# Converting float64 weights on Trainium2: the exponent is lowered on ScalarE, and one of VectorE's three steps goes

## The chip, the cores and the metric

One Trainium2 chip, of which this kernel uses one core. TensorE (PE) multiplies matrices, VectorE (DVE), ScalarE (ACT) and GpSimd (POOL) work element by element, and SyncE (SP) issues most transfers. Each engine works through its own list of instructions in order; semaphores make one wait for another. The metric is the time of one execution on the device in microseconds (us); lower is better.

## The reference

Pooled attention, then two feed-forward layers, over 8 x 576 = 4608 tokens of width 512:

```python
k_p, v_p = mean of k, v over groups of 8 positions
x = softmax(q @ k_p.T / 8) @ v_p
g, val = x @ w_gate, x @ w_val                     # 512 x 1536 each
x = (g * sigmoid(g) * val) @ w_out                 # 1536 x 512
h = x @ w_in                                       # 512 x 2048
out = (P(h) / (Q(h) + 1e-6)) @ w_out2              # 2048 x 512; P, Q small polynomials in h and |h|
```

The five weight matrices arrive in the accelerator's memory as float64; q, k and v are float32.

## The kernel before

Every matrix product is made of three products of TensorE's rounded float32 type: each float32 operand is split into a high part (the rounded value, by ScalarE) and a low part (the rest, by a subtraction), and `mm3` adds high x high, low x high and high x low. A product of one 128 x 128 weight block with 512 tokens is one matmul; 12 such matmuls (four blocks, three terms) are called *a product* below.

The tokens are worked on in nine blocks of 512. The program's stages, in order:

- **Start**: attention of block 0, while the first weights arrive.
- **Stage 0** (`j == 0`, L774 to L819): block 0 goes through the first feed-forward layer in 12 turns (`f`), each one of 128 hidden columns: the products `gp` (gate) and `vp` (value), then the output product `acc` of the turn before. Meanwhile attention for block 1 is placed in turns 5 to 11 (`place`). In this stage the weights of the first layer are converted as they are used: `first.step(6)` stands three times in a turn (L789, L796, L807), once for each of the turn's three weight tiles.
- **Stages 1 and 2**: blocks 1 and 2 in the same way, with the weights kept. GpSimd makes sums of the weights that a later stage wants; from stage 1 on, the second layer's weights are converted in half tiles (`Halves`, L176) and put back into memory.
- **Pair stage** (L902 to L976): the other six blocks, in three pairs of 12 turns, with weights streamed from memory; attention and the second layer's conversions go on beside.
- **The rest**: the output products of the pairs, and the second layer. No weights are converted any more.

A float64 is two 32-bit words. The conversion to float32 (`conversion`, L102) makes the float32's bits out of the high word's and adds the top bits of the low word:

1. `words()` on ScalarE: the magnitude of the high word, read as a float32, into tile `t` (L110); and the low word as an integer, times 2^-29 (L111), which leaves its top three bits.
2. `bits`, on VectorE: the maximum of `t` and a least value (L120), so that a tiny weight's exponent doesn't wrap; a shift left by 3 and a mask that drops the top two bits (L121); and `select` (L114), which takes the top two bits of the high word itself and joins them to the shifted rest.
3. GpSimd adds the low word's three bits (L117).

`Weights.step` (L143) keeps three tiles in flight, one in each part: it subtracts for the low half of the tile that is last (L149, VectorE), starts `words()` of a new one, runs the VectorE part for the one in the middle, and rounds the high half of the third (L165, ScalarE). So between L114 of a tile and its L149 there is GpSimd's addition and ScalarE's rounding, and the product that needs the tile's low half waits for L149. The names are those of the trace: `rawg`, `rawv`, `rawo` for the words of a gate, value and output tile, `tg`, `tv`, `to` for their `t`, `wg`, `wv`, `wo` for what is made of them, `rawi` and `rawo` with 256 columns for the half tiles. The `t` of some tiles and the loads of k, v and q share a pool of six buffers (`ldp`, tag `ld`), so a load waits until L114 has read an older `t`.

There are 36 conversions of 128 x 512 in the start and stage 0, and 64 of 128 x 256 from stage 1 to the end of the pair stage. In a half tile's turn `second.begin()`, `.middle()` and `.end()` hold ScalarE's words, VectorE's bits, and the split.

Of the kernel before, what the change touches and what calls it, by code (L numbers as in the profile page):

```python
# [10 lines left out]
F32 = mybir.dt.float32  # L11
F32R = mybir.dt.float32r
U32 = mybir.dt.uint32
AF = mybir.ActivationFunctionType
ALU = mybir.AluOpType
# [48 lines left out]
def attention_gated_rational(  # L64
# [4 lines left out]
    nc = tc.nc  # L69
# [11 lines left out]
    def f32(ap):  # L81
        return ap.bitcast(F32)
# [14 lines left out]

    LEAST = float(np.uint32(0x38000000).view(np.float32))  # L100

    def conversion(key, raw, n, spare, t=None):  # L102

        hi_word, lo_word = raw[:, :, 1], raw[:, :, 0]
        if t is None:
            t = ldp.tile([P, 512], F32, tag="ld", name=f"t{key}")[:, :n]
        tu = t.bitcast(U32)

        def words():
            nc.scalar.activation(t, hi_word.bitcast(F32), AF.Abs)  # L110
            nc.scalar.activation(lo_word, lo_word, AF.Copy, scale=2.0 ** -29)  # L111

        def select():
            nc.vector.scalar_tensor_tensor(  # L114
                hi_word, hi_word, 0xC0000000, tu, op0=ALU.bitwise_and, op1=ALU.bitwise_or
            )
            nc.gpsimd.tensor_tensor(tu if spare else hi_word, hi_word, lo_word, op=ALU.add)  # L117

        bits = [
            lambda: nc.vector.tensor_scalar(t, t, LEAST, None, op0=ALU.max),  # L120
            lambda: nc.vector.tensor_scalar(  # L121
                tu, tu, 3, 0x3FFFFFFF, op0=ALU.logical_shift_left, op1=ALU.bitwise_and
            ),
            select,
        ]
        return words, bits, t if spare else f32(hi_word)

    class Weights:
# [14 lines left out]
        def step(self, ahead, eng=None):  # L143
            begun = None
            middle, rounded, last = self.stages
            if last:
                key, spare, _, t = last
                w = self.done[key]
                (eng or nc.vector).tensor_tensor(w[:, 1, :], t, f32(w[:, 0, :]), op=ALU.subtract)  # L149
                live["w"] -= not spare  # L150
            if self.raws:
                key, raw, spare = self.raws.pop(0)
                words, bits, t = conversion(key, raw, 512, spare)
                words()
                begun = key, spare, bits, t
            if middle:
                for fn in middle[2]:
                    fn()
                live["w"] -= middle[1]
            if rounded:  # L160
                live["w"] += 1
                assert live["w"] <= WSLOTS
                key, t = rounded[0], rounded[3]
                w = self.done[key] = wslot(f"w{key}")
                nc.scalar.activation(w[:, 0, :], t, AF.Copy)  # L165
            self.stages = [begun, middle, rounded]
            while self.next < len(self.items) and len(self.raws) < ahead:
                if live["w"] + (self.next < self.spare or any(x and not x[1] for x in self.stages)) >= WSLOTS:
                    break
                self.load()  # L170
# [5 lines left out]
    class Halves:  # L176
# [26 lines left out]
        def begin(self, n=1, more=1):  # L203
            self.store()
            for _ in range(more):
                self.load()
            self.now = []
            for key, h, tile_, raw in [self.raw.pop(0) for _ in range(min(n, len(self.raw)))]:
                t = f32(tile_[:, 512:768])
                words, bits, _ = conversion(f"{key}_{h}", raw, 256, True, t)  # L210
                words()
                self.now.append((key, h, tile_, t, bits))
# [803 lines left out]
    def hidden_part(p, key, k):  # L1016
        while order_h and len(ahead) < 3:
            nxt = order_h[0]
            if nxt[0] != p and nxt[2] == 0 and k < NK - 1:
                break  # L1020
            ahead.append(hidden_sum(*order_h.pop(0)))
        t = ring_tile(f"h{p}{key}_{k}")
        split(t[:, 0, :], t[:, 1, :], ahead.pop(0))
        return t
# [3 lines left out]
    for p, (j1, j2) in enumerate(PAIRS):  # L1028
# [36 lines left out]
        for i, (ow, key) in enumerate(zip(O_ORDER, TOKENS)):  # L1065
# [5 lines left out]
            for k in range(NK):  # L1071
                t = hidden_part(p, key, k)
# [29 lines left out]
    with tc.tile_pool(name="p2", bufs=1, reuse_waits="tile") as p2:  # L1102
# [31 lines left out]
        for n, (j, f) in enumerate(its):  # L1134
# [11 lines left out]
            t = p2.tile([P, BLK], F32, tag="t", name=f"t{n}")  # L1146
# [93 lines left out]
```

## Time and profile before

| | us |
|---|---|
| median of 3 runs | 1798.62 (1796.67 to 1802.75) |
| the profiled execution: its own time | 1798.48 |
| the profiled execution: span from first to last instruction | 1796.7 |
| PE busy | 1743.1 (97%) |
| DVE busy | 1404.0 (78%) |
| ACT busy | 1135.4 (63%) |
| POOL busy | 345.4 (19%) |

Busy times are sums over the span; an engine that is busy for 78% of all the time can be busy for all of one stage. The ends of matmuls in the trace are modelled, so a PE that is shown busy may still be issuing less than it could. The mean granted clock of TensorE is 0.996 of 2.4 GHz.

### The profile page before, as it was taken

How to read it: one execution, taken by the hardware profiler on the slowest of the kernel's cores; microseconds unless marked ns; L12 is line 12 of the kernel's file. 1: busy time of each engine (PE TensorE's matmuls, PEld its weight loads, DVE VectorE, ACT ScalarE, POOL GpSimd, SP SyncE). 2: the span in 40 equal slices, each digit the busy share in tenths (PEclk: the TensorE clock that was granted, in tenths of full speed). 3: DMA queues.
4: the chain of work that ended last, by engine and by line, in shares of the span. 5: the costliest groups of instructions: out<-in, count | busy, mean ns of one | idle time of the engine just before them, and what ended most of it. 6: DMA issues, size and time to landing. Idle time of an engine off the chain costs nothing.

```text
span 1796.7 us, 23824 instructions
## 1 busy us (share of the span) xinstructions
PE 1743.1 (97%) x8212; PEld 1423.5 (79%) x8212; DVE 1404.0 (78%) x2333; ACT 1135.4 (63%) x1994; POOL 345.4 (19%) x492
## 2 busy tenths in 40 slices
PE   6898999999999999999999999999999999999998
PEld 5677877787887887887888788888888888888887
DVE  7997665548777676546777898989898989898987
ACT  5676455546665766435455676777677777767775
POOL 3344555542454344210000000000000000000000
PEclk9999999999999999999999999999999999999999
DMA  7631756559999898999826601010101010101000
GB/s 256 215 109 59 226 184 238 198 178 330 336 371 353 278 367 297 329 365 372 317 109 234 246 1 47 1 47 1 47 1 47 1 47 1 47 1 47 1 24 24
DMA packets 157464, 285.27 MB, mean 159 GB/s; under 512 B 12320, under 2 KB 78496, under 8 KB 156320
## 3 DMA queue, kind: packets, MB, share of 16 engines
q1 hardware_dynamic: 156624, 283.43, 44.8%
q8 instruction: 65, 1.06, 0.2%
q10 hardware_dynamic: 720, 0.33, 0.1%
q14 instruction: 55, 0.45, 0.1%
HBM read 194.58 MB, written 89.13 MB: 158 GB/s over the span
## 4 chain that ended last, share of the span: by engine, by line
PE 81%; DVE 5%; ACT 3%; issue 2%; POOL 1%; DMA 1%; POOLq 0%; DVEq 0%; ACTq 0%; SPq 0%
PE acco L256 22%; PE h L256 21%; PE ca L256 9%; PE ya L1083 5%; PE cc L256 5%; PE acc L256 3%; PE vp L256 3%; PE yc L1083 3%; PE gp L256 2%; PE cb L256 2%; PE pv L457 1%; PE yb L1083 1%; PE sc L368 1%; PE t L429 1%; DMA sw<-wd 0%
## 5 line engine op out<-in xcount | busy, mean ns | idle before, releaser
L256 PE MATMUL acco<-wo,gt 128*128 128x512 f32 x1728 | 417.3, 390 | 2.8 <-ACT gt L1170 2.4
L256 PE MATMUL h<-z,wi 128*128 128x512 f32 x1728 | 414.7, 389 | 0.0
L256 PEld LDWEIGHTS acco<-wo,gt 128*128 128x128 f32 x1728 | 325.3, 188 | 71.8 <-ACT gt L1170 3.2
L256 PEld LDWEIGHTS h<-z,wi 128*128 128x128 f32 x1728 | 324.4, 188 | 67.4
L1149 ACT ACTIVATE sq<-h 128x512 f32<-128x512 f32 x144 | 86.1, 598 | 197.3 <-PE h L256 197.3
L1156 DVE SCALAR_TENSOR_TENSOR w<-sq,neg,w 128x512 f32<-128x512 f32 x144 | 108.0, 750 | 48.2 <-ACT w L1150 48.2
L256 PE MATMUL vp<-x,wv 128*128 128x512 f32 x432 | 109.5, 401 | 6.2 <-DVE wv L149 6.2
L1166 DVE SCALAR_TENSOR_TENSOR g<-t,neg,e 128x512 f32<-128x512 f32 x144 | 108.3, 752 | 5.1
L1153 ACT ACTIVATE t<-h,neg 128x512 f32<-128x512 f32 x144 | 112.0, 778 | 0.0
L1162 DVE SCALAR_TENSOR_TENSOR t<-t,neg,h 128x512 f32<-128x512 f32 x144 | 107.7, 748 | 5.1
L256 PE MATMUL gp<-x,wg 128*128 128x512 f32 x432 | 108.0, 397 | 3.1 <-DVE wg L149 3.0
L1163 DVE SCALAR_TENSOR_TENSOR e<-w,ln 128x512 f32<-128x512 f32 x144 | 98.6, 685 | 13.5 <-ACT ln L1160 13.4
L1160 ACT ACTIVATE ln<-ln,lnb 128x512 f32<-128x512 f32 x144 | 104.3, 724 | 4.7
L256 PE MATMUL acc<-ht,wo 128*128 128x512 f32 x432 | 104.7, 391 | 0.0
L1170 ACT ACTIVATE gt<-g 128x512 fp32r<-128x512 f32 x144 | 90.8, 631 | 21.8 <-DVE g L1166 21.8
L1164 DVE SCALAR_TENSOR_TENSOR e<-e,ln 128x512 f32<-128x512 f32 x144 | 99.7, 692 | 5.0
L1150 ACT ACTIVATE w<-h,cab 128x512 f32<-128x512 f32 x144 | 98.3, 683 | 3.6 <-DVE e L1163 3.6
L256 PEld LDWEIGHTS vp<-x,wv 128*128 128x128 f32 x432 | 80.5, 191 | 25.3 <-DVE wv L149 8.7
L1171 DVE TENSOR_TENSOR gt<-g,gt 128x512 fp32r<-128x512 f32 x144 | 98.9, 687 | 1.9 <-ACT gt L1170 0.8
L1161 DVE TENSOR_TENSOR t<-t,h 128x512 f32<-128x512 f32 x144 | 98.2, 682 | 0.0
L256 PEld LDWEIGHTS gp<-x,wg 128*128 128x128 f32 x432 | 79.2, 188 | 22.8 <-DVE wg L149 5.1
L256 PEld LDWEIGHTS acc<-ht,wo 128*128 128x128 f32 x432 | 80.2, 188 | 16.7
(247 smaller groups left out, 3161.2 us busy)
## 6 DMA issues: line engine op xcount, KB each, us to landing
sw<-sd SPq DMA_DIRECT2D x72, 512.0 KB, 7.7
sw<-wd SPq DMA_DIRECT2D x36, 512.0 KB, 6.2
h<-hq SPq DMA_DIRECT2D x36, 512.0 KB, 7.8
sd<-sp SPq DMA_DIRECT2D x24, 512.0 KB, 4.3
sw<-vd SPq DMA_DIRECT2D x36, 256.0 KB, 7.8
hl<-h SPq DMA_DIRECT2D x18, 512.0 KB, 6.7
hr<-h SPq DMA_DIRECT2D x18, 512.0 KB, 9.7
out<-ob SPq DMA_DIRECT2D x36, 256.0 KB, 2.2
```

The lines of the kernel that those rows point to most:

```text
L256: nc.tensor.matmul(acc, st[:, lw, cols], mv[:, rw, mcols], start=first and i == 0, stop=last and i == n - 1, skip_group_check=seeded,)
L1083: nc.tensor.matmul(banks[q], w[:, lw, cols], t[:, rw, :], start=opened and k == 0 and m == 0, stop=k == NK - 1 and m == 2, skip_group_chec ...
L1150: nc.scalar.activation(w0, hps, AF.Abs, scale=cab[:, 4:5])
L1153: nc.scalar.activation(t, hps, AF.Identity, scale=neg[:, 3:4], bias=neg[:, 2:3])
L1156: nc.vector.scalar_tensor_tensor(w0, sq, neg[:, 5:6], w0, op0=ALU.mult, op1=ALU.add)
L1160: nc.scalar.activation(ln, ln, AF.Exp, scale=-1.0, bias=lnb)
L1161: nc.vector.tensor_tensor(t, t, hps, op=ALU.mult)
L1162: nc.vector.scalar_tensor_tensor(t, t, neg[:, 1:2], hps, op0=ALU.add, op1=ALU.mult)
L1163: nc.vector.scalar_tensor_tensor(e, w0, C1, ln, op0=ALU.add, op1=ALU.mult)
L1164: nc.vector.scalar_tensor_tensor(e, e, 2.0, ln, op0=ALU.subtract, op1=ALU.mult)
L1166: nc.vector.scalar_tensor_tensor(g, t, neg[:, 0:1], e, op0=ALU.add, op1=ALU.mult)
L1171: lambda gt=gt, g=g: nc.vector.tensor_tensor(gt[:, 1, :], g, f32(gt[:, 0, :]), op=ALU.subtract),
```

## The change

ScalarE's magnitude instruction gets a factor of 2^-112, so that the float32 it makes has its exponent lowered by 112. The float32's top two bits under the sign are then zero, and a value too small for it comes out as zero or tiny rather than wrapped: the maximum (L120) goes, the mask of L121 goes (a plain shift stays), and `select` takes the sign bit alone from the high word.

```diff
-    LEAST = float(np.uint32(0x38000000).view(np.float32))
+    REBIAS = 2.0 ** -112
...
         def words():
-            nc.scalar.activation(t, hi_word.bitcast(F32), AF.Abs)
+            nc.scalar.activation(t, hi_word.bitcast(F32), AF.Abs, scale=REBIAS)
             nc.scalar.activation(lo_word, lo_word, AF.Copy, scale=2.0 ** -29)
 
         def select():
             nc.vector.scalar_tensor_tensor(
-                hi_word, hi_word, 0xC0000000, tu, op0=ALU.bitwise_and, op1=ALU.bitwise_or
+                hi_word, hi_word, 0x80000000, tu, op0=ALU.bitwise_and, op1=ALU.bitwise_or
             )
...
         bits = [
-            lambda: nc.vector.tensor_scalar(t, t, LEAST, None, op0=ALU.max),
-            lambda: nc.vector.tensor_scalar(
-                tu, tu, 3, 0x3FFFFFFF, op0=ALU.logical_shift_left, op1=ALU.bitwise_and
-            ),
+            lambda: nc.vector.tensor_scalar(tu, tu, 3, None, op0=ALU.logical_shift_left),
             select,
         ]
```

No other instruction is added, removed or moved on any engine or queue: VectorE's list has 2231 rows instead of 2331, the 100 fewer being the L120 of the 100 conversions. The file is three lines shorter, so in the changed kernel the shift is L120, and lines after it have numbers lower by 3 (L149 is L146, L803 is L800). On VectorE, in the second turn of stage 0, there stood before:

```order
L149 TENSOR_TENSOR wv_640<-rawv_143,wv_640 128x512
L120 TENSOR_SCALAR tg_633<-tg_633 128x512
L121 TENSOR_SCALAR tg_633<-tg_633 128x512
L114 SCALAR_TENSOR_TENSOR rawg_255<-rawg_255,tg_633 128x512
L149 TENSOR_TENSOR wo_659<-rawo_145,wo_659 128x512
L120 TENSOR_SCALAR tv_652<-tv_652 128x512
L121 TENSOR_SCALAR tv_652<-tv_652 128x512
L114 SCALAR_TENSOR_TENSOR rawv_290<-rawv_290,tv_652 128x512
L803 TENSOR_TENSOR hh_1_676<-hh_1_676,vp_1_690 128x512
L149 TENSOR_TENSOR wg_686<-rawg_255,wg_686 128x512
```

and now:

```order
L146 TENSOR_TENSOR wv_634<-rawv_143,wv_634 128x512
L120 TENSOR_SCALAR tg_628<-tg_628 128x512
L114 SCALAR_TENSOR_TENSOR rawg_255<-rawg_255,tg_628 128x512
L146 TENSOR_TENSOR wo_652<-rawo_145,wo_652 128x512
L120 TENSOR_SCALAR tv_646<-tv_646 128x512
L114 SCALAR_TENSOR_TENSOR rawv_289<-rawv_289,tv_646 128x512
L800 TENSOR_TENSOR hh_1_669<-hh_1_669,vp_1_682 128x512
L146 TENSOR_TENSOR wg_678<-rawg_255,wg_678 128x512
```

Two of eight instructions before the product `hh` are gone, and the subtraction for `wo` is now followed by the shift of `tv` itself. On VectorE, in a turn of the pair stage, the half tile's part was:

```order
L863 TENSOR_TENSOR hq_4620<-hq_4620,cq_4560 128x512
L120 TENSOR_SCALAR rawo_4_0_4563<-rawo_4_0_4563 128x256
L121 TENSOR_SCALAR rawo_4_0_4563<-rawo_4_0_4563 128x256
L114 SCALAR_TENSOR_TENSOR rawo_4_0_4563<-rawo_4_0_4563 128x256
L287 TENSOR_REDUCE kr_4411<-k_1024_4549 128x64
```

and is now:

```order
L860 TENSOR_TENSOR hq_4566<-hq_4566,cq_4508 128x512
L120 TENSOR_SCALAR rawo_4_0_4511<-rawo_4_0_4511 128x256
L114 SCALAR_TENSOR_TENSOR rawo_4_0_4511<-rawo_4_0_4511 128x256
L284 TENSOR_REDUCE kr_4360<-k_1024_4497 128x64
```

Here one instruction of 128 x 256 is gone, between the last products of a hidden tile and the reductions of k.

## Rows read from the trace of the kernel before

Where busy time is shown by stretch, the columns are: stretch, its length, then for PE, PEld (weight loads), DVE, ACT and POOL the busy time with the number of instructions, the granted clock of TensorE, the share of the DMA engines' time, and GB/s.

**Rows 1.** Busy time by stretch: start and stage 0, stages 1 and 2, pair stage.
```profile
0.00:170.00 170.00, 137.15 (x703) 108.71 (x704) 149.59 (x279) 117.56 (x230) 68.43 (x79) 0.99 0.45 157
170.00:480.00 310.00, 303.75 (x1601) 243.90 (x1599) 194.77 (x372) 171.38 (x294) 146.93 (x239) 1.00 0.69 234
480.00:830.00 350.00, 343.57 (x1699) 279.05 (x1698) 222.03 (x427) 197.99 (x382) 130.03 (x175) 0.99 0.96 342
```

**Rows 2.** Chain that ended last, in order of time (start, length, what).
```profile
125.50 0.72 DVE wv L149
...
155.23 0.70 DVE hh L803
...
175.54 2.72 PE vp L256 x12
```

**Rows 3.** Busy time by stretch, turns 1 to 5, 8, 9, 10; columns as above.
```profile
43.00:94.70 51.70, 44.48 (x197) 33.33 (x196) 50.67 (x83) 33.20 (x56) 19.33 (x16) 1.00 0.61 205
...
121.86:132.60 10.74, 10.41 (x60) 8.15 (x58) 10.37 (x19) 10.21 (x17) 5.40 (x7) 1.00 0.15 49
132.60:146.56 13.96, 12.29 (x72) 9.74 (x71) 13.46 (x27) 13.32 (x22) 5.06 (x6) 1.00 0.20 67
146.56:156.58 10.02, 9.45 (x46) 7.38 (x43) 9.67 (x19) 8.34 (x14) 5.99 (x6) 1.00 0.00 0
```

**Rows 4.** PE in order of time; in brackets idle time before, and its releaser.
```profile
59.02 2.11 PE L256 MATMUL vp<-x,wv 128*128 128x512 f32 x8 [0.90 <-DVE wv L149]
...
111.42 0.46 PE L429 MATMUL t<-ident,p 64*128 64x64 f32 x4 [1.99 <-POOL p L404]
...
112.18 4.60 PE L256 MATMUL vp<-x,wv 128*128 128x512 f32 x12
...
125.89 3.03 PE L256 MATMUL vp<-x,wv 128*128 128x512 f32 x12
...
161.81 0.46 PE L429 MATMUL t<-ident,p 64*128 64x64 f32 x4 [2.35 <-POOL p L404]
```

**Rows 5.** DVE in order of time, parts of a turn of stage 0.
```profile
50.87 1.27 DVE L120 TENSOR_SCALAR tv<-tv 128x512 f32<-128x512 f32 x1
52.17 0.43 DVE L121 TENSOR_SCALAR tv<-tv 128x512 uint32<-128x512 uint32 x1
...
58.88 0.43 DVE L120 TENSOR_SCALAR tg<-tg 128x512 f32<-128x512 f32 x1
59.34 0.43 DVE L121 TENSOR_SCALAR tg<-tg 128x512 uint32<-128x512 uint32 x1
```

**Rows 6.** POOL in order of time, same turn.
```profile
50.48 1.37 POOL L117 TENSOR_TENSOR rawg<-rawg 128x512 uint32<-128x512 uint32 x1 [2.55 <-DVE rawg L114]
```

**Rows 7.** Line L120 on DVE, tiles tv, 37.9 to 162 us: ns min/median/max.
```profile
L120 DVE TENSOR_SCALAR tv<-tv x11: 414/1266/1268, 40.7 to 153.6; 128x512 f32<-128x512 f32 x11
```

**Rows 8.** Groups of DVE and ACT, start and stage 0 (busy us, mean ns).
```profile
L114 DVE SCALAR_TENSOR_TENSOR rawv<-rawv,tv 128x512 uint32<-128x512 uint32 x12 | 8.3, 694 | 0.4
...
L111 ACT ACTIVATE rawv<-rawv 128x512 uint32<-128x512 uint32 x12 | 8.1, 672 | 0.0
L110 ACT ACTIVATE tv<-rawv 128x512 f32<-128x512 f32 x12 | 8.0, 671 | 1.7 <-DVE rawo L114 1.7
```

**Rows 9.** Busy time of L120 alone, by stretch.
```profile
0.00:170.00 170.00, 21.81 (x36) 0.99 0.45 157
...
170.00:830.00 660.00, 21.55 (x64) 0.99 0.84 291
```

**Rows 10.** The half tiles: line L114, and DVE in a turn of the pair stage.
```profile
L114 DVE SCALAR_TENSOR_TENSOR rawi<-rawi x32: 425/427/1397, 174.6 to 807.6; 128x256 uint32<-128x256 uint32 x32
...
599.85 0.29 DVE L120 TENSOR_SCALAR rawi<-rawi 128x256 f32<-128x256 f32 x1
600.17 0.29 DVE L121 TENSOR_SCALAR rawi<-rawi 128x256 uint32<-128x256 uint32 x1
...
606.36 0.69 DVE L956 TENSOR_TENSOR cq<-cq,ca 128x512 f32<-128x512 f32 x1 [4.33 <-PE ca L256]
```

## The prediction

> **What bounds the kernel now.** I read the busy time by stretch first. Over the whole span TensorE is busy and VectorE is not, but the first stretch is another case: in the start and stage 0 VectorE is busy for 149.6 of 170 us, TensorE for 137.2 [rows 1]. After that TensorE is shown busy for all but 6.25 us of the 310 of stages 1 and 2, and all but 6.4 of the 350 of the pair stage [rows 1]. The second view is the chain that ended last: from 125.5 to 155.9 us every piece of it is a VectorE instruction, one behind the other, with issue gaps of some 0.02 us between; then it passes through ScalarE and GpSimd to TensorE, and stage 1 begins with products of 2.72 us, one behind the other [rows 2]. The third is the busy time of single turns of stage 0: turns 1 to 5 take 51.7 us, 10.34 each, and VectorE is busy for 50.67 of it, 98% [rows 3]. A turn holds three products, 3 x 2.72 = 8.16 us, so TensorE loses 2.2 us in each. The fourth, TensorE in order of time, says to whom: inside a product, between the matmuls that want only a tile's high half and those that want its low half, it waits for L149 of that tile, 0.90 us in the turn shown [rows 4]. L149 is late because its engine has a full list. So in stage 0, and there alone, VectorE's work is time of the kernel.
>
> **The change part by part.**
>
> *The maximum goes, in stage 0.* L120 was busy for 21.81 us there in 36 instructions [rows 9]. That isn't what is won. A plain L120 starts at 58.88 and its L121 at 59.34: 0.46 us of the list [rows 5]. The L120 of a `tv` tile is shown with 1.27 us [rows 5], and the eleven of them range from 414 to 1268 ns, half at 1266 or more [rows 7]. The long one runs from 50.87 to 52.14 while GpSimd's addition for the `rawg` tile runs from 50.48 to 51.85 [rows 6]: what is left after that addition, 0.3 us, is about a plain L120, so the rest, some 0.85 us, was a wait for GpSimd. With L120 gone the shift starts there instead, waits for the same addition, and ends 0.46 us earlier than it did, not 1.3. So I count 36 x 0.46 = 16.6 us, and the other 5.2 us as passed on to the next instruction. The Trainium skill has this as a rule: SBUF — State Buffer, section "SBUF: two separate sides", says that VectorE, in a two-port mode or with two inputs from SBUF, and GpSimd take one shared port pair as an exclusive lock for a whole instruction, and the other is blocked until it is free. By that rule the wait stays with whoever comes next, as counted; without it all of L120's busy time would be won, and the sum below would be 5.2 us larger.
>
> *The 16.6 us, place by place.* (a) Three conversions lie before the first product, where VectorE also waits for other things; of their 1.4 us I take 0.6. (b) Two lie in turn 0, in front of the `wg` that TensorE waits for: 0.9. (c) Fifteen lie in turns 1 to 5: 15 x 0.46 = 6.9, which makes a turn 10.34 - 1.38 = 8.96 us, still above TensorE's 8.16, so VectorE stays the bound and all of it is won. (d) Six lie in turns 6 and 7, with the first steps of attention; in turn 7 TensorE waits 1.99 us for GpSimd's softmax product, which waits for VectorE [rows 4], so I take all 2.7. (e) Nine lie in turns 8 to 10, worth 4.1 us of VectorE. But there ScalarE, which does the table changes of exponential and Silu beside its conversions, is busy for 10.21 of 10.74, 13.32 of 13.96 and 8.34 of 10.02 us [rows 3]: 2.85 us of room in all. TensorE in turn 8 is shown busy for 10.41 of 10.74 too. So I take 2.5 of the 4.1. (f) One lies in turn 11, where TensorE waits 2.35 us for the softmax of the turn [rows 4]; I take 0.5. Sum: 0.6 + 0.9 + 6.9 + 2.7 + 2.5 + 0.5 = 14.1 us.
>
> *The mask goes and the shift stays.* The shift with one operation isn't in this trace. Its nearest rows are L121 with two operations, 0.43 us, and L120 with one, 0.43 [rows 5]: they are alike, so I take no difference. The far bound is a VectorE instruction that runs at the slow rate, L114 with 0.694 [rows 8], 0.26 more; below, nothing can be won, since the two fast forms are equal.
>
> *ScalarE's factor.* L111 has a factor and takes 0.672, L110 has none and takes 0.671 [rows 8]: nothing, with 0.1 us either way as a generous bound that 36 times over would be 3.6 us of ScalarE and only matter in (e). `select` changes a constant: nothing.
>
> *The 64 half tiles.* L120 is busy for 21.55 us there [rows 9], 0.32 from start to start in the turn shown [rows 10]. I cost it at nothing: TensorE hides it. After such a conversion and a softmax sum VectorE stands idle for 4.33 us until TensorE is done [rows 10]. If that cover weren't there, the whole gain would be 64 x 0.32 = 20 us; but TensorE's shown idle time in both stretches is 12.7 us, and only a small part waits for VectorE. I allow 2 us either way, for turns in which the engines now meet in another order.
>
> *TensorE's clock.* In turn 7, after the wait of 1.99 us, the product `vp` takes 4.60 us instead of the 3.03 of the next turn [rows 4], the first being at 1.2 GHz, the second at 2.4. If the wait shrinks by the 1.38 us or more that VectorE is ahead, the fall may not come: up to 1.6 us more. I leave it out of the sum and in the range.
>
> *Loads.* Loads of k, v and q wait for L114 to free a buffer. L114 comes earlier, so they do too; the transfers have 0.61 of their time taken in turns 1 to 5 [rows 3], and about 0.70 when a turn is 8.96 us. Nothing.
>
> The sum is made against the profiled execution's 1798.48 us, which is 0.14 below the median of the runs, so the same serves for both: 1798.5 - 14.1 = **1784.4 us**.
>
> **The rivals.**
>
> *Another engine takes over at once.* TensorE's 8.16 us of 8.96 leave little room, and a VectorE that is no longer late must wait for `vp` at L803 in each turn, and for ScalarE's roundings. If each turn gave only half of what VectorE saves, the gain would be 7 us: 1791.5. For it: ScalarE in turns 8 to 10. Against it: in turns 1 to 5 ScalarE is busy for only 33.2 of 51.7 us [rows 3], and there alone 6.9 us lie.
>
> *Stage 0's gain is given back later.* The DMA engines are busy for 96% of the pair stage [rows 1]; if that stage ended when its transfers allow, whatever came before, the time would stay near 1798. Against it: its transfers are issued as buffers come free, turn by turn, so they begin earlier as well.
>
> *The change doesn't do what it says:* the plain shift runs at the slow rate. A conversion then saves 0.46 - 0.26 = 0.20 us, 36 of them 7 us at most: about 1792. Against it: L120 had one operation too and was fast.
>
> *Slower: the wait for GpSimd moves to a place that matters.* In the half tiles L114 takes 427 ns at the median but 1397 at most [rows 10], 0.97 more, when it meets GpSimd. Without L120 in front, other instructions meet GpSimd's work in 64 turns. To eat the 14.1 us and 5.4 more, TensorE would have to wait for it in 20 of the 64; with 32, at 31 us, the time would be 1815. It decides only where VectorE is the last that TensorE waits for. Against it: VectorE's idle times in that stage, such as the 4.33 us.
>
> **How the numbers follow.** A measurement of this kernel can tell about 0.3%, 5.4 us, from no change; faster therefore means below 1793.2. My forecast, a gain of 10 to 19 us, has 0.68. The first rival has 0.17, with gains of 4 to 10 us, so 0.14 of it is faster and 0.03 the same. The second has 0.08, all the same. The slow shift has 0.03: 0.02 faster, 0.01 the same. The slower rival has 0.04. Together faster 0.84, same 0.12, slower 0.04. The range begins at 1798.5 - 19.5 = 1779: the sum with the clock's 1.6, the half tiles' 2 and, in (e) and (f), the rest of VectorE's 2 us. It ends at 1792, which takes in the middle of the first rival and the slow shift; what lies outside is about 0.17.
>
> **What would show it.** Right: the second product of stage 1, at 175.5 [rows 2], begins about 14 us earlier; turns 1 to 5 take about 45 us together, with VectorE still busy for over 95% of them; the remaining shift of the `tv` tiles is the one shown with 1.27 us; from stage 1 on, the stretches are as long as before. In turns 8 to 10 ScalarE is busy nearly without a gap. Wrong: turns 1 to 5 at 48 us or more with gaps on VectorE (the first rival), a shift of 0.69 us without GpSimd beside it (the third), a stage 0 that is 14 us shorter with a pair stage longer by as much (the second), or TensorE waiting for L149 as long as before.

## The result, and the profile after

The changed kernel took 1781.62 us in the median of four runs (1779.47 to 1782.29); beside it the kernel before took 1799.45 (1796.67 to 1802.75). The ratio is 0.9898, with a 95% interval of 0.9879 to 0.9917: the change saves about 1%, some 18 us. The forecast was 1784.4, within 1779 to 1792. The profiled execution after took 1781.81 us, 16.67 less than the one before.

The page's first part, after:

```profile
span 1780.0 us, 23730 instructions
PE 1739.0 (98%) x8212; PEld 1422.3 (80%) x8212; DVE 1366.0 (77%) x2233; ACT 1134.4 (64%) x1994; POOL 342.0 (19%) x492
```

VectorE lost 38.0 us of busy time and the span lost 16.7. Less than half of what an engine stops doing came back as time. The busy time by stretch shows where (start and stage 0, then stages 1 and 2, then the pair stage, each cut where it now ends; columns as in [rows 1]):

```profile
0.00:157.00 157.00, 135.07 (x705) 109.08 (x706) 132.84 (x244) 116.81 (x230) 67.85 (x79) 1.00 0.48 170
157.00:470.00 313.00, 306.82 (x1624) 246.50 (x1622) 190.09 (x357) 172.65 (x298) 148.89 (x242) 1.00 0.70 237
470.00:815.00 345.00, 339.38 (x1677) 276.03 (x1676) 206.68 (x380) 198.56 (x382) 125.23 (x171) 1.00 0.96 343
```

Such cuts are round numbers. To book the difference I use events that both traces have: the start of the first `gp` matmul of each turn, of the first `cb` of the pair stage and of the first `ya` of what follows. Between these starts the two profiled executions took, in us:

| | before | after | difference | predicted |
|---|---|---|---|---|
| up to the first `gp` | 36.99 | 37.18 | +0.19 | -0.6 (a) |
| turn 0 | 5.81 | 5.81 | 0.00 | -0.9 (b) |
| turns 1 to 5 | 51.87 | 45.07 | -6.80 | -6.9 (c) |
| turns 6 and 7 | 27.19 | 22.81 | -4.38 | -2.7 (d) |
| turns 8 to 10 | 34.72 | 33.19 | -1.53 | -2.5 (e) |
| turn 11 | 16.08 | 15.18 | -0.90 | -0.5 (f) |
| stages 1 and 2 | 249.32 | 249.29 | -0.03 | 0 |
| pair stage | 408.73 | 405.07 | -3.66 | 0, 2 either way |
| the rest | 965.99 | 966.40 | +0.41 | 0 |

Stage 0 gave 13.4 of the 14.1 us that were forecast, and 3.7 us came from a stage that was to give nothing.

The single turns (1 to 5, 8, 9, 10), which answer to [rows 3]:

```profile
42.99:88.06 45.07, 43.53 (x197) 33.82 (x197) 44.54 (x68) 33.39 (x58) 19.18 (x16) 1.00 0.70 238
110.87:121.88 11.01, 10.38 (x60) 8.15 (x59) 9.30 (x18) 10.95 (x18) 5.72 (x7) 1.00 0.15 48
121.88:135.01 13.13, 12.25 (x72) 9.75 (x71) 12.70 (x25) 13.06 (x23) 6.34 (x7) 1.00 0.21 71
135.01:144.06 9.05, 9.05 (x47) 7.47 (x43) 7.16 (x15) 8.29 (x14) 4.77 (x5) 1.00 0.00 0
```

In turns 1 to 5 VectorE is busy for 44.54 of 45.07 us, 99%: it still sets the pace, with 15 instructions fewer. The transfers' share rose from 0.61 to 0.70, as worked out. In turns 8 to 10 VectorE has room now (29.16 of 33.19), and TensorE is shown busy for 31.68.

VectorE in order of time, in a turn of stage 0, with GpSimd's addition beside it:

```profile
56.42 0.42 DVE L120 TENSOR_SCALAR tg<-tg 128x512 uint32<-128x512 uint32 x1
56.87 0.69 DVE L114 SCALAR_TENSOR_TENSOR rawg<-rawg,tg 128x512 uint32<-128x512 uint32 x1
57.48 0.69 DVE L146 TENSOR_TENSOR wo<-rawo,wo 128x512 fp32r<-128x512 f32 x1
58.08 1.27 DVE L120 TENSOR_SCALAR tv<-tv 128x512 uint32<-128x512 uint32 x1
59.38 0.69 DVE L114 SCALAR_TENSOR_TENSOR rawv<-rawv,tv 128x512 uint32<-128x512 uint32 x1
```

```profile
57.70 1.37 POOL L117 TENSOR_TENSOR rawg<-rawg 128x512 uint32<-128x512 uint32 x1 [2.08 <-DVE rawg L114]
```

L120 is the shift now. The one of `tg` takes 0.42 us, and the one of `tv` has inherited the 1.27 us that the maximum showed [rows 5]: it starts at 58.08, beside an addition that ends at 59.07, and ends 0.28 us after that. All twelve `tv` tiles (min/median/max, ns) look like [rows 7]:

```profile
L120 DVE TENSOR_SCALAR tg<-tg x12: 374/418/478, 22.3 to 137.4; 128x512 uint32<-128x512 uint32 x12
L120 DVE TENSOR_SCALAR tv<-tv x12: 411/1264/1268, 29.3 to 140.3; 128x512 uint32<-128x512 uint32 x12
```

TensorE in order of time, three places of stage 0:

```profile
56.55 2.11 PE L253 MATMUL vp<-x,wv 128*128 128x512 f32 x8 [0.29 <-DVE wv L146]
...
102.01 0.46 PE L426 MATMUL t<-ident,p 64*128 64x64 f32 x4 [0.61 <-POOL p L401]
102.77 3.02 PE L253 MATMUL vp<-x,wv 128*128 128x512 f32 x12
...
148.42 0.46 PE L426 MATMUL t<-ident,p 64*128 64x64 f32 x4 [1.48 <-POOL p L401]
```

The wait for the low half of `wv` fell from 0.90 to 0.29 us [rows 4]. In turn 7 the wait for the softmax product fell from 1.99 to 0.61, by as much as three maxima take (1.38 us), and the product behind it takes 3.02 us, not 4.60: TensorE's granted clock was 1.00 over it, which is 2.4 GHz, and 0.63 before the change.

The chain that ended last, pieces of it in order of time:

```profile
43.61 0.68 DVE wg L146
...
99.58 0.67 DVE sm L398
...
117.28 1.28 ACT L386
...
162.13 2.72 PE vp L253 x12
```

From 43.6 to 100.7 us nearly every piece is VectorE's. From there to stage 1 the chain runs through GpSimd, ScalarE and TensorE, where before it was VectorE's from 125.5, where that view begins, up to 155.9 [rows 2]. So turns 8 to 11 have passed to other engines. The second product of stage 1 begins 13.41 us earlier, at 162.13 against 175.54.

### The profile page after: what moved, and what is told of

Read it like the earlier page. It is cut to its first block, busy times and chain, and to the rows that moved or that the text cites. A ratio compares the mean times of both kernels' runs of the same rounds, so it can differ in the third digit from the quotient of the medians.

```text
span 1780.0 us, 23730 instructions
## 1 busy us (share of the span) xinstructions
PE 1739.0 (98%) x8212; PEld 1422.3 (80%) x8212; DVE 1366.0 (77%) x2233; ACT 1134.4 (64%) x1994; POOL 342.0 (19%) x492
## 3 DMA queue, kind: packets, MB, share of 16 engines
q8 instruction: 65, 1.06, 0.2%
## 4 chain that ended last, share of the span: by engine, by line
PE 84%; DVE 6%; ACT 3%; issue 2%; DMA 2%; POOL 2%; SPq 0%; POOLq 0%; DVEq 0%; ACTq 0%
PE acco L253 22%; PE h L253 22%; PE ca L253 9%; PE ya L1080 5%; PE cc L253 5%; PE vp L253 3%; PE acc L253 3%; PE gp L253 3%; PE yc L1080 3%; PE cb L253 2%; PE pv L454 2%; PE sc L365 1%; PE yb L1080 1%; PE t L426 1%; ACT L386 1%
## 5 line engine op out<-in xcount | busy, mean ns | idle before, releaser
L1160 DVE SCALAR_TENSOR_TENSOR e<-w,ln 128x512 f32<-128x512 f32 x144 | 98.6, 685 | 13.5 <-ACT ln L1157 13.4
L253 PEld LDWEIGHTS acc<-ht,wo 128*128 128x128 f32 x432 | 80.2, 188 | 16.7
```

The costliest lines, as they stand in the source:

```text
L253: nc.tensor.matmul(acc, st[:, lw, cols], mv[:, rw, mcols], start=first and i == 0, stop=last and i == n - 1, skip_group_check=seeded,)
L1160: nc.vector.scalar_tensor_tensor(e, w0, C1, ln, op0=ALU.add, op1=ALU.mult)
```

## The experiments

My theory after the result: in stage 0 a maximum is worth what it takes of VectorE's list, 0.4 to 0.5 us, and not what it shows, because a wait for GpSimd is passed on; and the pair stage's 3.7 us come from the half tiles, at one place. Rivals: the pair stage's part is inherited from the engines meeting in another order; the mask matters; ScalarE holds turns 8 to 10. The booked places of all runs stand here together (us):

| | median | turns 1-5 | 6-7 | 8-10 | 11 | pair stage |
|---|---|---|---|---|---|---|
| whole tiles only | 1783.24 | 45.05 | 22.82 | 33.15 | 15.22 | 409.10 |
| half tiles only | 1797.41 | 51.85 | 27.17 | 34.75 | 16.06 | 406.94 |
| mask kept | 1781.03 | 45.07 | 22.82 | 33.21 | 16.78 | 405.16 |
| maximum twice | 1816.86 | 57.84 | 29.85 | 39.16 | 19.61 | 410.56 |
| no table changes | 1781.88 | 45.30 | 22.86 | 32.64 | 14.37 | 407.09 |
| no magnitude | 1779.28 | 45.32 | 22.86 | 32.66 | 14.66 | 405.54 |
| before, no addition | 1787.00 | 45.47 | 22.70 | 32.68 | 15.61 | 408.94 |
| low bits in the shift | 1772.39 | 43.41 | 21.33 | 32.30 | 16.89 | 400.57 |
| the same, half tiles only | 1779.13 | 45.06 | 22.83 | 33.14 | 15.22 | 404.14 |
| the same, whole tiles only | 1778.18 | 43.15 | 21.33 | 32.28 | 16.96 | 405.58 |

Stages 1 and 2 took 249.1 to 249.8 us in every one.

### The two kinds of tiles apart

On the kernel before: the new conversion for one kind, the old one for the other. ScalarE's factor and the constant of `select` go by the same condition.

```diff
+        if n == 512:                    # n == 256 in the other kernel
+            bits = [
+                lambda: nc.vector.tensor_scalar(tu, tu, 3, None, op0=ALU.logical_shift_left),
+                select,
+            ]
```

> The new conversion for the 36 whole tiles of the start and stage 0 only; the 64 half tiles keep maximum and mask. Theory (VectorE's list is the bound in stage 0 and, for a few instructions, where a new pair of blocks begins in the pair stage; the two gains are separate): stage 1's first product comes 13.4 us earlier than before, as with the whole change, and the pair stage is as long as before, so 1799.45 - 13.4 = 1786 us (1785 to 1787.5). Rival (the 3.7 us that the pair stage won come from the stages before meeting in another order, not from its own half tiles): the pair stage is shorter here too, 1781.6 to 1783 us.

Measured: 1783.24 us (1783.16 to 1784.93) beside 1799.03, a ratio of 0.9915 (0.9901 to 0.993). Stage 0 has its whole gain, turn by turn as after; the pair stage takes 409.10 us, as long as before. The median is 1.8 us under the range that was expected, and near the rival's: in the profiled execution the first `gp` started 1.0 us earlier than before, and what follows the pair stage took 1.5 us less, so the rows and not the median decide.

> The new conversion for the 64 half tiles only; the whole tiles of stage 0 keep maximum and mask. Theory: stage 0 as before; the pair stage wins about 3.7 us, all of it in the turns where a pair ends and the next begins (2 us of it between the product cb of turns 12 and 13): 1799.45 - 3.7 = 1795.8 us (1794.5 to 1797). Rival (order of meeting): the pair stage is as long as before, 1798.5 to 1800.5 us.

Measured: 1797.41 us (1795.03 to 1799.23), a ratio of 0.9991 (0.9981 to 1.0). Stage 0 is as before; the pair stage is 1.8 us shorter, half of what was expected. The median misses its range as well, and by the interval, which ends at 1.0, it is hardly clear of no change.

What follows: the pair stage's gain isn't inherited from stage 0, since the whole tiles alone don't bring it. It needs the half tiles. But these alone brought 1.8 us and not 3.7, which the section on the seam below takes up.

### The mask kept

```diff
-            lambda: nc.vector.tensor_scalar(tu, tu, 3, None, op0=ALU.logical_shift_left),
+            lambda: nc.vector.tensor_scalar(
+                tu, tu, 3, 0x7FFFFFFF, op0=ALU.logical_shift_left, op1=ALU.bitwise_and
+            ),
```

> The whole change, but the shift keeps a second operation, a mask with 0x7FFFFFFF that changes no bit of the value that is used. Theory: an instruction with two operations takes as long as one with one, so the time is that of the change, 1781.6 us (1780 to 1783), and the shift's shortest form takes 0.41 to 0.43 us. Rival (the dropped mask is part of the gain): 0.02 us or more per shift are lost again, 36 of them on the path make 0.7 us at 0.43 against 0.41, and more if the two-operation form is slower still: 1783 us or more.

Measured: 1781.03 us (1780.74 to 1786.0), a ratio of 0.9907 (0.9891 to 0.9923). The shift with a mask takes 377/419/476 ns for `tg`, the plain one 374/418/478, and turns 1 to 10 agree with those after within 0.02 us by group. What follows: the mask was free, and its going brings nothing; the whole gain is the maximum's.

### The maximum twice

On the kernel before, to price one maximum from the other side.

```diff
             lambda: nc.vector.tensor_scalar(t, t, LEAST, None, op0=ALU.max),
+            lambda: nc.vector.tensor_scalar(t, t, LEAST, None, op0=ALU.max),
```

> The kernel before, with the maximum done twice. Theory (a VectorE instruction costs its own 0.46 us of the list, and the wait for GpSimd is paid once by whoever comes first): turns 1 to 5 grow from 10.34 to 11.72 us each, stage 0 by 36 x 0.46 = 16.6 us less what lies before the first product, 15 to 16 us, the pair stage by about 3: 1799.45 + 18.5 = 1818 us (1815 to 1821); of the two maxima of a tv tile the first takes 1.27 us and the second 0.41. Rival (the maximum costs what its mean busy time shows, 0.61 us, since it is slow by itself on some tiles): turns 1 to 5 grow to 12.2 us, 36 x 0.61 = 21.8 us in stage 0, 1824 us or more, and both maxima of a tv tile take 1.27 us.

Measured: 1816.86 us (1814.65 to 1819.1), a ratio of 1.01 (1.0085 to 1.0115). The two maxima of the `tv` tiles (min/median/max, ns):

```profile
L120 DVE TENSOR_SCALAR tv<-tv x12: 411/1264/1270, 31.1 to 170.5; 128x512 f32<-128x512 f32 x12
L121 DVE TENSOR_SCALAR tv<-tv x12: 426/427/428, 31.5 to 170.9; 128x512 f32<-128x512 f32 x12
```

The same operation on the same tile costs 1264 ns when it comes first and 427 when it comes second. So the long time isn't the operation's; it is the wait for GpSimd that is running its addition, and the first that comes pays it. What one costs is read from turns 2 to 5, where VectorE was the bound and TensorE's granted clock 1.00 in all three kernels; before, with the maximum twice, and after the change:

```profile
53.54:94.67 41.13, 35.77 (x161) 26.79 (x159) 40.31 (x66) 26.62 (x45) 15.44 (x13) 1.00 0.62 209
```

```profile
57.63:104.29 46.66, 35.79 (x161) 26.79 (x159) 45.41 (x78) 26.09 (x44) 14.79 (x12) 1.00 0.56 187
```

```profile
52.48:88.06 35.58, 34.63 (x162) 27.10 (x160) 35.17 (x54) 26.56 (x47) 14.81 (x13) 1.00 0.72 245
```

Twelve maxima cost 5.53 us when added and gave 5.55 when removed, 0.46 each both ways. Had each cost its mean busy time of 21.81 / 36 = 0.61 us [rows 9], it would be 7.3. The other turns don't give a price: in turns 0, 9 and 11 of this kernel the granted clock fell to 0.81 to 0.83, which it hadn't before, so their 0.99, 4.10 and 3.53 us more are in part the clock's.

### The addition left out

On the kernel before, GpSimd's addition is left out for the whole tiles; their three lowest bits are then missing.

```diff
-                hi_word, hi_word, 0xC0000000, tu, op0=ALU.bitwise_and, op1=ALU.bitwise_or
+                tu if spare and n == 512 else hi_word, hi_word, 0xC0000000, tu, ...
             )
-            nc.gpsimd.tensor_tensor(tu if spare else hi_word, hi_word, lo_word, op=ALU.add)
+            if n == 256:
+                nc.gpsimd.tensor_tensor(tu if spare else hi_word, hi_word, lo_word, op=ALU.add)
```

> The kernel before, with GpSimd's addition of the low word's three bits left out for the 36 whole tiles (their last three bits are missing). Theory (the long maxima of the tv tiles and the long subtractions for wg are waits for that addition): all of the maxima take 0.41 to 0.48 us, the subtractions for wg 0.69 instead of 1.21; a turn loses 0.85 + 0.53 us of VectorE's list, turns 1 to 5 shrink from 51.9 to about 45 us, and the time to 1787 (1784 to 1790). Rival (these instructions are long by themselves, by their place in memory): the maxima of tv stay at 1.27 us, turns 1 to 5 within 1 us of 51.9, and the time within 3 us of 1799.

Measured: 1787.0 us (1784.56 to 1789.33), a ratio of 0.9935 (0.9918 to 0.9951). The maximum, which is L121 in this file:

```profile
L121 DVE TENSOR_SCALAR tv<-tv x12: 417/422/423, 29.4 to 140.4; 128x512 f32<-128x512 f32 x12
```

With no addition beside it none of the twelve is long. All maxima are still there, and yet turns 1 to 5 take 45.47 us, nearly as few as after the change:

```profile
43.14:88.61 45.47, 43.46 (x196) 33.80 (x196) 44.35 (x84) 32.53 (x58) 0.00 (x0) 1.00 0.67 233
```

VectorE is busy there for 6.3 us less than before [rows 3], with the same instructions. So it is VectorE's list that became shorter, and not only the way of a tile through GpSimd. What follows: an addition that runs on another engine cost turns 1 to 5 nearly as much, by the waits for it, as the maxima did (6.4 us against 6.8), and the change left these waits in place. The Trainium skill, SBUF — State Buffer, section "SBUF: two separate sides", says that VectorE in its two-port modes, or with two inputs from SBUF, and GpSimd hold their shared port pair as a lock for a whole instruction, and that the other is blocked meanwhile. The two runs agree: 1264 ns with the addition beside it, 427 and 422 without.

### ScalarE freed in turns 8 to 10

On the changed kernel. The first takes the table changes away, by a copy in place of the Silu of block 0, so the output isn't the reference's; the second takes the magnitude instruction away, since VectorE's shift can read the high word itself and mask its sign.

```diff
-            nc.scalar.activation(hh, gp, AF.Silu)
+            nc.scalar.activation(hh, gp, AF.Silu if j else AF.Copy)
```

> The change, with a plain copy in place of the Silu of stage 0, so that ScalarE never changes its table in that stage (the gate of the first block is left out, and the output is not the reference's). Theory (in turns 8 to 10 ScalarE is what kept 2.6 of VectorE's 4.1 us from counting): without six table changes of 1.28 us the three turns shrink from 33.2 us to what TensorE needs, 31 to 32; turns 1 to 5, which hold no table change, stay at 45 us; with turn 11 in all 1.5 to 3 us less, 1779 to 1780 us. Rival (TensorE's own work is what is left in those turns): turns 8 to 10 stay within 0.5 us of 33.2, and the time at 1781 to 1782 us.

Measured: 1781.88 us (1778.47 to 1783.54) beside 1799.61, a ratio of 0.9899 (0.9885 to 0.9914). Turns 8, 9 and 10 by busy time:

```profile
110.04:121.08 11.04, 10.42 (x60) 8.15 (x58) 10.33 (x19) 9.09 (x18) 5.71 (x7) 1.00 0.15 47
121.08:133.63 12.55, 12.26 (x72) 9.74 (x70) 12.15 (x24) 9.88 (x20) 6.35 (x7) 1.00 0.21 74
133.63:142.68 9.05, 9.05 (x46) 7.47 (x43) 8.20 (x16) 5.93 (x12) 4.77 (x5) 1.00 0.00 0
```

ScalarE is busy for 24.9 us of them, 7.4 less than after, and the turns take 32.64 us, 0.55 less. TensorE's 31.7 us are most of what is left. The time is the rival's; the 1.5 to 3 us that the theory asked for didn't come.

```diff
-            nc.scalar.activation(t, hi_word.bitcast(F32), AF.Abs, scale=REBIAS)
...
-                hi_word, hi_word, 0x80000000, tu, op0=ALU.bitwise_and, op1=ALU.bitwise_or
+                hi_word, hi_word, 0xC0000000, tu, op0=ALU.bitwise_and, op1=ALU.bitwise_or
...
-            lambda: nc.vector.tensor_scalar(tu, tu, 3, None, op0=ALU.logical_shift_left),
+            lambda: nc.vector.tensor_scalar(
+                tu, hi_word, 3, 0x3FFFFFFF, op0=ALU.logical_shift_left, op1=ALU.bitwise_and
+            ),
```

> The change, with ScalarE's magnitude left out: VectorE shifts the high word itself by 3 and masks its top two bits, and joins the top two bits as before (this holds for weights that are zero or above 2^-126). 100 ScalarE instructions go, 36 of them of 0.57 us each in stage 0. Theory (ScalarE is the bound in turns 8 to 10 and nowhere else; a shift from a word in two is as fast): turns 1 to 5 stay at 45 us, turns 8 to 10 shrink by 1.2 to 2 us, 1779.5 to 1780.5 us. Rival (the shift falls to the slow form, since its source is strided): 0.69 instead of 0.43 us per shift, turns 1 to 5 grow by 15 x 0.26 = 3.9 us, and the time to about 1788 us.

Measured: 1779.28 us (1778.05 to 1780.04), a ratio of 0.9887 (0.9872 to 0.9902). The shift reads every second word and is as fast as the one that reads a packed tile:

```profile
L119 DVE TENSOR_SCALAR tg<-rawg x12: 374/418/482, 22.4 to 135.8; 128x512 uint32<-128x512 uint32 x12
```

Turns 8 to 10 gain 0.53 us, where 1.2 to 2 were expected, and that is all of turns 1 to 10 that becomes shorter. What follows from both: ScalarE, however full, held turns 8 to 10 by half a microsecond only. In turn 8 neither gained, and there TensorE's one wait is for GpSimd's softmax product, before, then after the change:

```profile
125.20 0.66 PE L429 MATMUL t<-ident,p 128*128 128x128 f32 x4 [0.33 <-POOL p L404]
```

```profile
114.52 0.66 PE L426 MATMUL t<-ident,p 128*128 128x128 f32 x4 [0.63 <-POOL p L401]
```

Without the additions for whole tiles on GpSimd, on the kernel before, this wait is 0.16 us, and in the kernel of the next section, which has none, it is gone.

### The low bits joined in the shift

The waits for GpSimd are what is left on VectorE's list. On the changed kernel, ScalarE truncates the low word's bits, the shift takes them in with a second operation, and GpSimd's addition goes. The shift is then a form with two inputs from memory, like L114, which takes 0.694 us [rows 8].

```diff
-            nc.scalar.activation(lo_word, lo_word, AF.Copy, scale=2.0 ** -29)
+            nc.scalar.activation(lo_word, lo_word, AF.Copy, scale=2.0 ** -29, bias=-0.5)
...
-            lambda: nc.vector.tensor_scalar(tu, tu, 3, None, op0=ALU.logical_shift_left),
+            lambda: nc.vector.scalar_tensor_tensor(
+                tu, tu, 3, lo_word, op0=ALU.logical_shift_left, op1=ALU.bitwise_or
+            ),
...
-            nc.gpsimd.tensor_tensor(tu if spare else hi_word, hi_word, lo_word, op=ALU.add)
```

> The change, with GpSimd's addition gone for all tiles: ScalarE rounds the low word's three bits down (bias -0.5), and VectorE joins them in the instruction that shifts, which gets a second input and so the slow form, 0.69 us. Theory: per conversion VectorE pays 0.15 us more from start to start (0.61 instead of 0.46), but no longer waits for GpSimd, 1.38 us per turn of three conversions; a turn needs 8.74 + 0.45 - 1.38 = 7.8 us of VectorE, less than TensorE's 8.16. Turns 1 to 5 shrink from 45.1 to 41 to 42 us, stage 0 in all by 4 to 6 us: 1776 to 1778 us. Rival (the waits aren't GpSimd's, or the slow shift costs what they did): turns 1 to 5 grow by 15 x 0.15 = 2.3 us, 1784 us.

Measured: 1772.39 us (1770.42 to 1773.89), a ratio of 0.9849 (0.9834 to 0.9863) to the kernel before: faster than both, and 3.6 us under the range that was expected. Busy time from 43 to 84 us (most of turns 1 to 5) and from 100 to 140 us, and two groups of VectorE:

```profile
43.00:84.00 41.00, 39.78 (x174) 32.17 (x173) 40.41 (x66) 31.45 (x55) 0.00 (x0) 1.00 0.70 239
100.00:140.00 40.00, 39.40 (x223) 31.73 (x222) 37.09 (x66) 36.99 (x60) 9.10 (x12) 1.00 0.17 57
```

```profile
L119 DVE SCALAR_TENSOR_TENSOR tv<-tv,rawv 128x512 uint32<-128x512 uint32 x12 | 8.2, 684 | 0.0
...
L801 DVE TENSOR_TENSOR hh<-hh,vp 128x512 f32<-128x512 f32 x12 | 8.2, 684 | 5.4 <-PE vp L254 5.3
```

The shift costs 684 ns instead of some 420, and no `tv` tile waits for GpSimd any more. Turns 2 to 5 take 8.20, 8.16, 8.16 and 8.90 us: the three products of 2.72, TensorE's own time, and VectorE now waits for TensorE at `hh`. Turn 1 took 9.99 us, so turns 1 to 5 came to 43.41 and not to the 41 to 42 expected. From 100 to 140 us TensorE is busy for 39.40 of 40.00. Turns 8 to 10, at 32.30, are near their floor, which tells what step (e) had left to win: after the change 0.9 us. More than was expected came from the pair stage, 4.50 us less than after the change; the section on the seam tells how much of it is the clock's.

### The same for one kind of tile

`joined` decides by the tile's size whether it is converted as in the last kernel or as in the changed one.

```diff
+        joined = n == 256               # n == 512 in the other kernel
...
+        if joined:
+            bits[0] = lambda: nc.vector.scalar_tensor_tensor(
+                tu, tu, 3, lo_word, op0=ALU.logical_shift_left, op1=ALU.bitwise_or
+            )
```

> The change, with the low bits joined in the shift (no addition on GpSimd) for the 64 half tiles only; the whole tiles as in the change. Theory (where a pair of blocks ends, VectorE and GpSimd are late and TensorE's clock falls for it; the addition is part of that): stage 0 as in the change, the pair stage 400 to 402 us instead of 405.1, with turn 12 to 13 at about 14 us and no fall of the clock there; 1781.6 - 4.5 = 1777 us (1775.5 to 1778.5). Rival (the pair stage of the run with all tiles joined was short because its stage 0 was): the pair stage stays at 405 us, 1781 to 1782 us.

Measured: 1779.13 us (1775.94 to 1780.83) beside 1800.29, a ratio of 0.9882 (0.9867 to 0.9897); the pair stage took 404.14 us. The clock fell after all, so the pair stage missed its 400 to 402 us, and the time its range.

> The change, with the low bits joined in the shift for the 36 whole tiles only; the half tiles as in the change. Theory: turns 2 to 5 at TensorE's 8.16 us each (8.9 with the first scores) as in the run with all tiles joined, the pair stage at 405 us as in the change; stage 0 from the first product to stage 1's is 121 us if the clock falls in turn 11 and 119.4 if not, against 122.1: 1778 to 1780.5 us. Rival: the pair stage falls to 401 us with it, 1773 to 1775 us.

Measured: 1778.18 us (1775.49 to 1779.96), a ratio of 0.9874 (0.9857 to 0.989); turns 2 to 5 take the 8.2 to 8.9 us of the kernel with both. What follows: in the profiled executions each kind brings a part of its own, the whole tiles in stage 0 and the half tiles 0.93 us in the pair stage. By the intervals of the ratios neither alone is clear of the changed kernel; the kernel with both is, and it is the fastest of all that ran. It gained 9.2 us on the changed kernel, where the two alone gained 2.5 and 3.4; at the seam below, it and the kernel with half tiles only are 3.1 us of clock apart.

### The seam between two pairs

The pair stage's 36 turns took the same time before and after, within 0.08 us each, but for four: turns 0, 12 and 24, each the first of a pair (14.80, then 14.44; 18.81, then 16.76; 11.09, then 10.31), and turn 33 (10.93, then 10.59). Turn 33 is no seam. There TensorE waits for streamed weights to land, before the change:

```profile
807.76 1.62 PE L256 MATMUL ca<-x2b,sw 128*128 128x512 f32 x6 [1.13 <-DMA sw<-wd]
```

It took 10.29 us with the maximum twice and 11.37 without table changes, so its 0.34 us isn't booked to the half tiles.

Turn 12 is the largest. It begins with the new pair's `cb` of `x1b` and goes on to products of that pair's `x1t`, whose split into halves (L94, two of 2.20 us together) stands on a list of VectorE without idle time that holds the three half tiles of turns 11 and 12 as well. TensorE in order of time from the end of that wait to the end of the turn, first before, then after:

```profile
577.94 0.79 PE L256 MATMUL ca<-x1t,sw 128*128 128x512 f32 x1 [1.05 <-DVE x1t L94]
578.66 1.99 PE L368 MATMUL sc<-kr,q 64*128 64x72 f32 x16
...
586.95 1.52 PE L256 MATMUL cb<-x1b,sw 128*128 128x512 f32 x6
```

```profile
563.06 0.50 PE L253 MATMUL ca<-x1t,sw 128*128 128x512 f32 x1 [1.06 <-DVE x1t L94]
563.49 1.11 PE L365 MATMUL sc<-kr,q 64*128 64x72 f32 x16
...
571.02 1.54 PE L253 MATMUL cb<-x1b,sw 128*128 128x512 f32 x6
```

Then the kernel with low bits in the shift for all tiles, and the one that has it for the half tiles only:

```profile
558.65 0.49 PE L254 MATMUL ca<-x1t,sw 128*128 128x512 f32 x1 [1.05 <-DVE x1t L94]
559.08 1.12 PE L366 MATMUL sc<-kr,q 64*128 64x72 f32 x16
...
565.03 1.54 PE L254 MATMUL cb<-x1b,sw 128*128 128x512 f32 x6
```

```profile
561.63 0.80 PE L259 MATMUL ca<-x1t,sw 128*128 128x512 f32 x1 [1.05 <-DVE x1t L94]
562.36 1.99 PE L371 MATMUL sc<-kr,q 64*128 64x72 f32 x16
...
571.09 1.54 PE L259 MATMUL cb<-x1b,sw 128*128 128x512 f32 x6
```

The same wait of 1.05 us stands ahead in all four. The 16 small matmuls behind it take 1.11 us in two of them and 1.99 in the others, which is TensorE at 1.2 GHz (before the change the granted clock was 0.50 from 578 to 582 us). From the matmul after the wait to the next turn's `cb` it is 9.01 us before, 7.96 after, 6.38 and 9.46. The last two have the same instructions there and the same two waits (0.48 and 1.05 us): 3.1 us between them are the clock alone. Over the 8 us that begin 0.35 us behind the matmul's start the granted clock was 1.00 in the one and 0.60 in the other.

So of the 2.05 us that turn 12 lost with the change, 1.00 lies ahead of the matmul (9.80 to 8.80 us: a shorter list on VectorE, by three maxima of 0.32 us) and 1.05 lies behind it, in the clock. That also places the kernel with half tiles only: its waits in the turn were those after the change (0.27, 0.72, 1.05 us), its clock came back later (granted 0.59 over the 8 us that begin 0.8 us ahead of the matmul, after the change 0.79), and turn 12 took 18.34 us. The changed kernel without table changes, whose tiles are all converted in the new way, is such a case too: 8.81 us ahead of the matmul, 9.17 behind it, 17.98 in all. So the 1.00 goes with the half tiles in every run, and the 1.05 doesn't.

## Why the prediction was right, and where not

*The bound, and the price of a maximum: right.* VectorE's list set turns 1 to 7, and a maximum there is worth 0.46 us, not the 0.61 that it shows on average: twelve of them made 5.53 and 5.55 us in turns 2 to 5. That the wait for GpSimd is passed on was an inference from one place of the trace; the maximum twice (1264 and 427 ns) and the addition left out (422) show it. That stage 0 as a whole came to 13.4 us against 14.1 is in part luck: (a), (b), (c) and (e) gave 2.8 us less than forecast, (d) and (f) 2.1 more, 1.6 of them the clock's.

*(a) and (b), 1.5 us: not there.* Turn 0 took 5.81 us both times. Its two products follow each other without a gap, so VectorE was not late in it. What the two maxima in front of `wg` are worth came out in turn 1, where the wait for `wg` fell from 0.96 to 0.16 us: so (c)'s 6.80 holds it already. (b) and (c) together were forecast at 7.8 and gave 6.80. For (a) nothing can be told: the first `gp` started between 35.6 and 38.1 us in the profiled executions of nearly the same start (39.65 with the maximum twice).

*(d), 2.7 us: it gave 4.38*, because the fall of the clock in turn 7 didn't come. The 1.6 us of it stood in the range, and 2.7 + 1.6 is nearly what was measured.

*(e), 2.5 us: it gave 1.53, and its reason was for the most part wrong.* I took ScalarE's 2.85 us of room as the limit. As forecast, ScalarE is busy nearly without a gap in these turns (32.30 of 33.19 us); but freed of 7.4 us of work it gave 0.55 us more, so a full engine was not by itself what held the turns. The limit was in the same rows: TensorE's idle time in turns 8 to 10 was 34.72 - 32.15 = 2.57 us [rows 3], and it was 0.33 in turn 8, where nothing was won (11.01 after 10.74). There TensorE's wait for GpSimd's softmax product grew from 0.33 to 0.63 us, and the wait was gone where GpSimd had no additions; why it grew stays open.

*(f), 0.5 us: it gave 0.90*, but the turn took 15.18 to 16.78 us in executions that have the same list there, as the clock fell or not. This is no test.

*The half tiles, "I cost it at nothing: TensorE hides it": the term that was mis-sized.* The pair stage gave 3.66 us, outside the 2 that I had allowed. Of these 1.05 are the clock in turn 12 and 0.34 a load in turn 33, which the runs don't tie to the half tiles; the other 2.3 are theirs, at the three seams. The medians allow as much: 1.6 us for the half tiles alone, and some 3 from the whole tiles alone (0.9915) to the change (0.9898), with intervals that overlap. The cover was read from a turn in the middle of a pair, where VectorE stands idle for 4.33 us [rows 10], and there it holds: 32 turns didn't change. It isn't there at the seams, where VectorE's list has no gap, and in turn 12 the clock's fall can cost as much again as being late. I wrote that only a small part of TensorE's idle time there waits for VectorE and did not look at where that part lies.

*The mask and ScalarE's factor, nothing each: right.* With a mask 419 ns, without 418; the magnitude takes 668 to 670 ns in the mean with its factor, 671 without [rows 8]. The Trainium skill, ScalarE: Activation LUTs, section "Rules for kernel authors", tells to give maxima and multiplications to VectorE rather than ScalarE. Here the multiplication rides on an instruction that ScalarE runs in any case, and by these rows it is free.

*The rivals.* No other engine took over in turns 1 to 5, which came to 45.07 us where 48 would have told for it. Nothing was given back in the pair stage. The plain shift is fast. Waits for GpSimd at new places cost nothing that shows: the pair stage became shorter.

The profiled executions differ by 16.7 us and the medians by 17.8. The start differs by up to 2.5 us, and what follows the pair stage by up to 2.1, between the profiled executions, so the runs don't ask for a cause of the 1.1 us.

## What to carry to other kernels

Price a removed instruction by the space that it takes in its engine's list next to a neighbour that doesn't wait, not by its busy time: a wait that it shows passes to the instruction behind it. Read for each place how long the engine that the result waits for is idle, since that caps what a turn can give at the same clock; another engine's fullness alone doesn't tell. A cover read in one turn of a loop says nothing of the first and last turns: look at the seams by themselves.

## What the hardware showed that was not expected

- Two executions with the same instructions and the same waits of 0.48 and 1.05 us had TensorE's granted clock at 1.00 and at 0.60 over the 8 us that follow, which was worth 3.1 us. Which of them a kernel gets isn't set by these waits alone: after the change, with half tiles only and without table changes the waits were alike too (0.27, 0.70 to 0.72 and 1.05 to 1.06 us), and what follows in the turn took 7.96, 9.53 and 9.17 us. What sets it stays open.
- A shift of 128 x 512 words that reads every second word took 418 ns in the median, as long as one that reads a packed tile.
- An operation with two inputs, slower by itself (684 ns against 418), in place of one that waits for GpSimd beside it, took turns 1 to 5 from 45.07 to 43.15 us (whole tiles only), since the waits went with the addition.
